# Full-width numerators and a matmul queue that stays in its row mode, in a linear-attention plus FFN kernel

## Chip, cores, metric

The kernel runs on one core of one Trainium2 chip. The metric is the device time of one execution in microseconds (us), as a median over runs. Runs of the kernel before lie within about 1 us of their median. All runs compared here are of the same ("fast") state unless a line says otherwise.

## The reference

Per batch (8) and head (8), queries, keys and values of 576 tokens x 64 go through a feature map and linear attention; the heads are joined to 4608 tokens x 512 and go through an FFN with a squared relu.

```python
def phi(x):
    proj = np.einsum('bhsd,df->bhsf', x, w_phi)            # 64 -> 128 features
    proj = proj - np.max(np.abs(proj), axis=-1, keepdims=True)
    return np.concatenate([np.exp(proj), np.exp(-proj)], axis=-1)
q_p, k_p = phi(q), phi(k)
kv  = np.einsum('bhsf,bhsd->bhfd', k_p, v)
num = np.einsum('bhsf,bhfd->bhsd', q_p, kv)
den = np.einsum('bhsf,bhf->bhs', q_p, np.sum(k_p, axis=2))[..., None] + 1e-06
x   = (num / den) ...                                     # (4608, 512)
h   = np.maximum(x @ w_in, 0.0)                           # d_ff = 2048
out = h * h @ w_out
```

## The kernel before

The kernel is a list of operations with keys (priorities), durations and dependencies. A planner in Python simulates the engines while the program is built and fixes the order of the instructions on each engine. The chip then runs that fixed order.

PE, the tensor engine, works in three shapes here: the FFN and the attention numerators contract over 128 rows; the projections of k and q and the k-v products contract over 64 rows (`rows=64`), two of them side by side in the array; and numerators of a lone half tile of 64 tokens use 128 rows x 64 columns ("column tiled"). The planner charges 96 ns when the row mode changes and nothing for a change of columns:

```python
    SWITCH = 96
    ...                                     # order(): PE picks the ready op of lowest key
                skip = []
                while q:
                    it = heapq.heappop(q)
                    o = it[2]
                    if not can(o):          # its PSUM banks or other buffers are not free
                        skip.append(it)
                        continue
    ...
                    if o.rows is not None:
                        if rows[e] not in (None, o.rows):
                            end += self.SWITCH
                        rows[e] = o.rows
```

PSUM, where PE's results land, is used as 8 banks (`r_one`). Attention may hold 6 at a time (`NATT = 6`), and a projection takes two, because it is written so that the two halves of the array write to different ones.

```python
    NATT, LEAD, DUE, SPAN = 6, 3, 34, 28
    r_one = ring("one", 8, [P, 512], F32, ps)
    r_att = Ring(list(range(NATT)))
    MARGIN = 300                            # added to the plan's latency of every eviction
    ...
            w, qg = banks(2), [Buf(r_qph), Buf(r_qph)]      # a q projection
    ...
            p_ = pe(kk, nj * 108, fn, tq + [o_wphi], w + [qT] + qg, 64)
```

Per batch there are 9 columns of 64 tokens: four pairs (`nj = 2`) and one single (`nj = 1`). The numerator of a single has 64 stationary columns and writes 64 PSUM partitions:

```python
            lo, hi_ = g0 % 2 * 64, (g0 % 2 + nj) * 64
    ...
                def nd(c, w=w, lo=lo, hi_=hi_):
                    return w.t.rearrange("t (h c) -> t h c", h=4)[lo:hi_, :, c]
                def fn(s, nd=nd, qg=qg, lo=lo, hi_=hi_, r=r):
                    for z in range(4):
                        h = 4 * r + z
                        nc.tensor.matmul(
                            out=nd(slice(0, D + 1))[:, z],
                            lhsT=qg[s].t.rearrange("f pr hi p -> f (pr hi p)")[
                                :, h * (hi_ - lo) : (h + 1) * (hi_ - lo)],
                            rhs=kv[r][0].t[:, z % 2, z // 2, s, :], ...)
```

An FFN unit is four 128x512 matmuls, 0.86 us. Attention operations become ready some three units before their key.

Of the kernel before, what the change touches and what calls it, by code (L numbers as in the profile page):

```python
# [17 lines left out]
class Buf:  # L18
# [5 lines left out]
    def can(self):  # L24
        free = self.ring.free
        return bool(free) if self.want is None else self.want in free
# [19 lines left out]
class Plan:  # L46
# [28 lines left out]

    SWITCH = 96

    def order(self):
        ready = {e: [] for e in sorted({o.eng for o in self.ops}, key=lambda e: (e != "x", e))}
        busy = {e: 0.0 for e in ready}  # L80
        rows = {e: None for e in ready}
        for o in self.ops:
            if o.n == 0:
                heapq.heappush(ready[o.eng], (o.key, o.seq, o))
        ev, now, done = [], 0.0, []

        def can(o):
            new = [x for x in o.bufs if x.slot is None]
            return all(x.can() and len(x.ring.free) >= sum(y.ring is x.ring for y in new)
                       for x in new)  # L90

        while True:
            for e, q in ready.items():
                if busy[e] > now:
                    continue
                skip = []
                while q:
                    it = heapq.heappop(q)
                    o = it[2]
                    if not can(o):  # L100
                        skip.append(it)
                        continue
                    for x in o.bufs:
                        if x.slot is None:
                            x.take()
                    o.start = now
                    end, lat = now + o.cost, o.lat
# [4 lines that stand above are left out]
                    busy[e] = end  # L112
                    done.append(o)
                    same = [d for d in o.next if d.eng == e]
                    other = [d for d in o.next if d.eng != e]
                    for i, (t, what) in enumerate((
                            (end, ()), (end + 60, same), (end + lat, other),
                            (end + lat, None))):
                        heapq.heappush(ev, (t, 4 * o.seq + i, o, what))
                    break  # L120
                for it in skip:
                    heapq.heappush(q, it)
                if busy[e] <= now and e in self.idle and self.idle[e][2].start is None:
                    cost, fn, _ = self.idle[e]
                    o = Op()
                    o.eng, o.fn, o.start, o.cost, o.key = e, fn, now, cost(now), 1e9
                    busy[e] = now + o.cost
                    done.append(o)
                    heapq.heappush(ev, (busy[e], -len(done), o, ()))
            if not ev:  # L130
                break
            now = ev[0][0]
            while ev and ev[0][0] <= now:
                _, _, o, what = heapq.heappop(ev)
                if what is None:
                    for x in o.bufs:
                        x.left -= 1
                        if x.left == 0:
                            x.ring.free.append(x.slot)
                    continue  # L140
                for d in what:
                    d.n -= 1
                    if d.n == 0:
                        heapq.heappush(ready[d.eng], (d.key, d.seq, d))
        assert all(o.start is not None for o in self.ops)
        self.span = now
        return done
# [10 lines left out]
def kernel(  # L158
# [12 lines left out]
    B, H, S, D = q.shape  # L171
    Fd = w_phi.shape[1]
    DM, DF = moe_w_in.shape
    P = 128
# [73 lines left out]
    def banks(n):  # L248

        w = [Buf(r_one) for _ in range(n)]  # L250
        for x in w:
            x.token = Buf(r_att)
        return w
# [25 lines left out]
    def begin():  # L279
# [5 lines left out]
        out=scrap[:, 4:8], in_=scrap[:, 0:4], func=ACT.Exp), [o_begin])  # L285
# [56 lines left out]
    def attention(b, x, key):  # L342
# [41 lines left out]
        if b:  # L384
            d = pl.op("x", 1000, key(2), None, tq)
            gates[b] = pool(key(2), 100, lambda: nc.gpsimd.tensor_copy(
                out=gate, in_=qT.t[:1, M - 1, P - 8 :]), [d], [qT])
# [4 lines left out]
        if b:  # L392
            def fn():
                nc.gpsimd.memset(va[0].t[:, :, D], 1.0)
                nc.gpsimd.tensor_copy(out=va[0].t[:, :, :D], in_=xv.t)
# [5 lines left out]
        for g, (u0, n) in enumerate(GRP):  # L401
            kk = key(2 + 8 * g)
            w = banks(2)
            c = n * 64
# [54 lines left out]
            for s_, (y, sg) in enumerate(zip(va, (-1.0, 1.0))):  # L459
# [4 lines left out]
                o = act(kk - 1, 2 * n, fn, d1, [y, mk])  # L464
# [11 lines left out]
        while g0 < (b + 1) * NJ:  # L476
            j0 = jord[b % 2][g0 - b * NJ]
            nj = 1 if j0 == NJ - 1 else 2
# [4 lines left out]
        for hf in range(2):  # L483
            t = Buf(r_kv)
            w = banks(2)

            def kvp(w, hi):
                return w[hi].t.rearrange("f (i c) -> f i c", i=4)[:, :, : D + 1]
            ops = []
            for prl in range(2):  # L490
                pr = 2 * hf + prl
# [17 lines left out]
            o = []  # L509
            for hi in range(2):  # L510
                kk = key(KV_AT[1] + 8 * hf + 6 if b else 20)
                if b or hi:
                    o.append(act(kk, 260, lambda w=w, t=t, hi=hi: nc.scalar.activation(
                        out=t.t[:, hi].rearrange("f pr s c -> f (pr s) c"),
                        in_=kvp(w, hi), func=ACT.Copy), ops, w + [t]))
                else:
                    o.append(dve(kk, 260, lambda w=w, t=t, hi=hi: nc.vector.tensor_copy(
                        out=t.t[:, hi].rearrange("f pr s c -> f (pr s) c"),
                        in_=kvp(w, hi)), ops, w + [t]))
# [5 lines left out]
        for i, (g0, j0, nj) in enumerate(order_j):  # L525
            lo, hi_ = g0 % 2 * 64, (g0 % 2 + nj) * 64
            kk = key(Q2_AT[b > 0][i])
            w, qg = banks(2), [Buf(r_qph), Buf(r_qph)]
# [15 lines left out]
            qe = []  # L544
            for bk in range(2):
                for t, sg in zip(qg, (1.0, -1.0)):
                    def fn(w=w, t=t, sg=sg, nj=nj, bk=bk):
                        nc.scalar.activation(  # L548
                            out=t.t.rearrange("f pr hi p -> f (pr hi p)")[:, : nj * 512].rearrange(
                                "f (r b c) -> f b r c", r=2, b=2)[:, bk],  # L550
                            in_=w[bk].t[:, : nj * 256].rearrange("f (r c) -> f r c", r=2),
                            func=ACT.Exp, scale=sg)
                    qe.append(act(kk, nj * 256, fn, [p_], [w[bk], t]))

# [2 lines left out]
            w, m0, mq, em = banks(2), Buf(r_m0), Buf(r_mq), Buf(r_em)  # L557

            def fn(w=w, j0=j0, nj=nj):
# [12 lines left out]
                out=m0.t[:, bk, : 2 * nj],  # L572
                in_=w[bk].t[:, : nj * 256].rearrange("x (i f) -> x i f", f=Fd),
# [23 lines left out]
            c, tt = tile_of[n2]  # L597
# [8 lines left out]
            for r in range(2):  # L606
                w, = banks(1)
                hs = slice(4 * r, 4 * r + 4)

                def nd(c, w=w, lo=lo, hi_=hi_):  # L610
                    return w.t.rearrange("t (h c) -> t h c", h=4)[lo:hi_, :, c]

                def fn(s, nd=nd, qg=qg, lo=lo, hi_=hi_, r=r):
                    for z in range(4):
                        h = 4 * r + z
                        nc.tensor.matmul(  # L616
                            out=nd(slice(0, D + 1))[:, z],
                            lhsT=qg[s].t.rearrange("f pr hi p -> f (pr hi p)")[
                                :, h * (hi_ - lo) : (h + 1) * (hi_ - lo)],
                            rhs=kv[r][0].t[:, z % 2, z // 2, s, :],  # L620
                            start=(s == 0 and z == 0), stop=True, skip_group_check=True)
                bs = [w, rd, xo, kv[r][0]]
                p_ = pe(kk, 132, lambda fn=fn: fn(0), [o_em] + qe + kv[r][1], bs + [qg[0]])

                def sc(nd=nd, em=em, lo=lo, hi_=hi_, hs=hs):
                    x = nd(slice(0, D + 1))
                    nc.vector.tensor_tensor(  # L627
                        out=x, in0=x, in1=em.t[lo:hi_, hs].to_broadcast(list(x.shape)),
                        op=ALU.mult)
                dk = kk - 20  # L630
                d_ = dve(dk, 260, sc, [p_, o_em], [w, em])
                p_ = pe(dk, 132, lambda fn=fn: fn(1), [d_], bs + [qg[1]])
                d_ = dve(dk, 50, lambda nd=nd, rd=rd, lo=lo, hi_=hi_, hs=hs:
                    nc.vector.reciprocal(out=rd.t[lo:hi_, hs], in_=nd(D)), [p_], [w, rd])

                def fn(nd=nd, rd=rd, xo=xo, lo=lo, hi_=hi_, hs=hs):
                    x = nd(slice(0, D))
                    nc.vector.tensor_tensor(  # L638
                        out=xo.t[lo:hi_].rearrange("t (h d) -> t h d", h=H)[:, hs],
                        in0=x, in1=rd.t[lo:hi_, hs].to_broadcast(list(x.shape)), op=ALU.mult)  # L640
                parts.append(dve(dk, 250, fn, [d_], [w, rd, xo]))
            nds.append(p_)
            if hi_ == P and b == 0:
                w, = banks(1)
# [159 lines left out]
```

## Time and profile before

| | before |
|---|---|
| time, median of 3 | 383.3 us (382.87 to 383.75) |
| first matmul on wout (its load has landed) | 49.5 us into the span |
| last 64-row matmul (end of the projections) | 302.9 us |
| changes of row mode in the whole trace | 212 |
| changes of columns alone | 47 |

PE is busy nearly throughout; at first it fills its idle time with matmuls on `ones` whose result is not used. Once wout has landed, PE's own stream sets the time. "Busy" is not "useful", though: PE's records overlap, so a drained array is not seen as idle. It is seen in the start times. The timeline of PE before, where columns are start, duration, engine, line, operation, shapes and count:

```profile
66.83 0.44 PE L616 MATMUL one<-kv_sb,qph 128*64 128x65 bf16 x8
67.20 1.04 PE L708 MATMUL one<-wout,h 128*128 128x512 bf16 x4
68.17 0.39 PE L538 MATMUL one<-qT,wphi 64*128 64x256 bf16 x4
...
152.57 0.41 PE L616 MATMUL one<-kv_sb,qph 128*128 128x65 bf16 x8
152.81 1.02 PE L708 MATMUL one<-wout,h 128*128 128x512 bf16 x4
153.77 0.39 PE L538 MATMUL one<-qT,wphi 64*128 64x256 bf16 x4
...
165.46 0.40 PE L412 MATMUL one<-wphi,kT 64*128 64x128 bf16 x8
165.79 1.04 PE L679 MATMUL one<-xT,win 128*128 128x512 bf16 x4
166.76 0.40 PE L412 MATMUL one<-wphi,kT 64*128 64x128 bf16 x8
167.09 1.04 PE L679 MATMUL one<-xT,win 128*128 128x512 bf16 x4
168.06 0.29 PE L412 MATMUL one<-wphi,kT 64*128 64x128 bf16 x4
168.28 4.49 PE L679 MATMUL one<-xT,win 128*128 128x512 bf16 x20
```

Read the starts. Four 512-column matmuls take 4 x 0.216 = 0.86 us; but from 152.81 to the 64-row work at 153.77 it is 0.96, and from 67.20 to 68.17 it is 0.97: 0.1 us went into the change of mode. Eight column-tiled numerators at 66.83 take 0.37 us to the next start, eight full ones at 152.57 only 0.24. And at 165 to 168 us three k projections stand alone between single FFN units: six changes of mode within 3 us.

The two forms of numerator, and of their weight loads, in the groups by form of the kernel before (after the bar: busy us and mean ns; then idle time before them):

```profile
L616 PE MATMUL one<-kv_sb,qph 128*128 128x65 bf16 x512 | 28.5, 195 | 1.5 <-DVE one L627 1.4
L616 PE MATMUL one<-kv_sb,qph 128*64 128x65 bf16 x128 | 9.1, 200 | 0.0
...
L616 PEld LDWEIGHTS <-qph 128*128 128x128 bf16 x512 | 23.6, 98 | 13.6 <-issue 2.9
L616 PEld LDWEIGHTS <-qph 128*64 128x64 bf16 x128 | 6.1, 110 | 8.6 <-issue 8.5
```

The durations look alike (195 and 200 ns): the cost is not in the matmul but around it. The Trainium skill, "TensorEngine Tiling (Array Packing)", Restrictions and Gotchas, says that column tiling excludes Fast Weight Load; the 64-column loads at 110 ns against 98 for full ones fit that, but weakly: the full loads of the filler matmuls average 106, and nothing here shows the mode bit.

### The profile page before, as it was taken

To read this page: it belongs to the slowest core of one execution; us is meant where nothing else is said; L and a number is where in the kernel's file an instruction comes from. 1 tells how busy PE (TensorE), PEld (TensorE's weight loads), DVE (VectorE), ACT (ScalarE), POOL (GpSimd) and SP (SyncE) were. 2 spreads that over 40 slices of the span, in tenths; PEclk is the share of its full clock that TensorE was granted. 3 is DMA by queue.
4 is the path that set the end of the run, shared out by engine and by line. 5 is a ranking of instruction groups with operands and counts; after the bars stand their busy time and mean duration, and the time that the engine had idled before them with its cause. 6 is when DMAs were issued, how large, how long until landed. Compare 5 with 4: busy or idle time off the path is not lost.

```text
span 382.5 us, 10585 instructions
## 1 busy us (share of the span) xinstructions
PE 366.7 (96%) x4194; PEld 200.9 (53%) x4194; DVE 247.7 (65%) x554; ACT 244.4 (64%) x485; POOL 185.9 (49%) x317
## 2 busy tenths in 40 slices
PE   8989999978999999999999999999999999999994
PEld 8868857544544454545543544455446444444442
DVE  1857894899279738973699488956895843333221
ACT  3785788649972986489758974996399733333300
POOL 8533766507890986079728674677446420000000
PEclk9998999999999999999999999999999999999998
DMA  7999994257944595459665946495631422112123
GB/s 114 213 208 205 162 174 73 48 91 133 195 50 89 91 217 62 80 105 202 99 85 109 169 85 104 91 196 102 105 77 30 71 55 49 35 29 55 27 64 75
DMA packets 70721, 40.41 MB, mean 106 GB/s; under 512 B 51088, under 2 KB 65552, under 8 KB 70672
## 3 DMA queue, kind: packets, MB, share of 16 engines
q1 hardware_dynamic: 55360, 21.38, 31.2%
q0 software_dynamic: 15312, 18.35, 29.4%
q8 instruction: 33, 0.54, 0.6%
q14 instruction: 16, 0.13, 0.1%
HBM read 36.77 MB, written 9.44 MB: 121 GB/s over the span
## 4 chain that ended last, share of the span: by engine, by line
PE 74%; DMA 11%; DVE 9%; issue 3%; POOL 1%; DVEq 0%; POOLq 0%
PE one L708 32%; PE one L679 25%; DMA wout<-in_moe_w_out_dram 8%; PE one L616 5%; PE one L500 5%; DVE mk L423 4%; DVE ksh L433 3%; PE one L538 3%; DMA xv<-in_v_dram 2%; PE one L567 2%; PE one L412 2%; DVE ot L715 1%; DVE xo L638 1%; POOL va L467 1%; DVE one L627 1%
## 5 line engine op out<-in xcount | busy, mean ns | idle before, releaser
L687 POOL TENSOR_TENSOR h<-hr 128x512 bf16<-128x512 bf16 x112 | 115.2, 1042 | 83.7 <-ACT hr L684 81.7
L679 PE MATMUL one<-xT,win 128*128 128x512 bf16 (+2 forms) x704 | 144.2, 341 | 2.8 <-DVE ksh L433 2.8
L708 PE MATMUL one<-wout,h 128*128 128x512 bf16 x576 | 144.5, 380 | 0.8 <-DMA wout<-in_moe_w_out_dram 0.5
L684 ACT ACTIVATE hr<-one 128x512 bf16<-128x512 f32 x144 | 84.5, 603 | 67.7 <-PE one L679 59.8
L548 ACT ACTIVATE qph<-one 128x512 bf16<-128x512 f32 (+1 forms) x160 | 77.9, 563 | 19.5 <-PE one L538 19.3
L679 PEld LDWEIGHTS <-win 128*128 128x128 bf16 x704 | 59.2, 98 | 54.6 <-issue 3.5
L708 PEld LDWEIGHTS <-h 128*128 128x128 bf16 x576 | 51.0, 98 | 56.6 <-issue 1.4
L441 ACT ACTIVATE kph<-ksh 128x1024 bf16<-128x1024 f32 (+1 forms) x70 | 64.8, 964 | 19.7 <-DVE ksh L433 19.2
L571 DVE TENSOR_REDUCE m<-one 128x4 f32<-128x512 f32 (+1 forms) x80 | 47.9, 630 | 41.7 <-PE one L567 24.9
L423 DVE TENSOR_REDUCE mk<-one 128x4 f32<-128x512 f32 (+1 forms) x80 | 49.7, 627 | 8.3 <-PE one L412 8.2
L433 DVE TENSOR_TENSOR ksh<-one,mk 128x512 f32<-128x512 f32 (+1 forms) x70 | 44.7, 638 | 3.8
L715 DVE COPY ot<-one 128x512 f32<-128x512 f32 x36 | 24.7, 685 | 28.2 <-PE one L708 28.0
L580 POOL COPY mq<-m 64x4 f32<-64x4 f32 x144 | 26.5, 184 | 32.0 <-DVE m L571 27.3
L616 PEld LDWEIGHTS <-qph 128*128 128x128 bf16 (+1 forms) x640 | 29.7, 100 | 22.2 <-issue 11.3
L616 PE MATMUL one<-kv_sb,qph 128*128 128x65 bf16 (+1 forms) x640 | 36.9, 196 | 1.5 <-DVE one L627 1.4
L627 DVE TENSOR_TENSOR one<-one,em 128x260 f32<-128x260 f32 (+1 forms) x80 | 31.5, 429 | 5.8 <-PE one L616 2.3
L638 DVE TENSOR_TENSOR xo<-one,rden 128x256 bf16<-128x256 f32 (+1 forms) x80 | 31.7, 419 | 0.8
L690 DVE TENSOR_TENSOR h<-hr 128x512 bf16<-128x512 bf16 x32 | 13.5, 423 | 24.4 <-ACT hr L684 24.4
L323 PE MATMUL one<-ones 128*128 128x128 bf16 x316 | 24.0, 236 | 1.1 <-DVE scrap L281 1.1
L500 PE MATMUL one<-va,kph 64*128 64x65 bf16 x1152 | 22.8, 191 | 0.9 <-issue 0.9
L500 PEld LDWEIGHTS <-kph 64*128 64x128 bf16 x1152 | 20.5, 94 | 4.3 <-issue 3.3
L323 PEld LDWEIGHTS <-ones 128*128 128x128 bf16 x316 | 20.6, 106 | 2.5 <-DVE scrap L281 1.1
(43 smaller groups left out, 184.5 us busy)
## 6 DMA issues: line engine op xcount, KB each, us to landing
out_dram<-ot SPq DMA_DIRECT2D x72, 128.0 KB, 2.4
xk<-in_k_dram POOLq DMA_DIRECT2D x7, 576.0 KB, 6.1
xq<-in_q_dram POOLq DMA_DIRECT2D x7, 576.0 KB, 9.8
xv<-in_v_dram POOLq DMA_DIRECT2D x7, 576.0 KB, 12.2
win<-in_moe_w_in_dram POOLq DMA_DIRECT2D x1, 2048.0 KB, 18.5
wout<-in_moe_w_out_dram POOLq DMA_DIRECT2D x1, 2048.0 KB, 32.4
xk<-in_k_dram POOLq DMA_DIRECT2D x2, 288.0 KB, 5.6
xq<-in_q_dram POOLq DMA_DIRECT2D x2, 288.0 KB, 7.6
```

The source lines that it names most:

```text
L323: nc.tensor.matmul(out=r_one.tiles[7][:, :P], lhsT=ones, rhs=ones, start=True, stop=True)
L423: nc.vector.tensor_reduce(out=mk.t[:, e, ms], in_=wv(e), axis=AX.X, op=ALU.max, apply_absolute_value=True)
L433: nc.vector.tensor_tensor(out=ksh.t[:, e, : n // 2, :], in0=wv(e), in1=mk.t[:, e, ms].to_broadcast([P, n // 2, Fd]), op=ALU.subtract)
L441: nc.scalar.activation(out=t.t[:, :, : n // 2, :].rearrange("x e i f -> x e (i f)"), in_=ksh.t[:, :, : n // 2, :].rearrange("x e i f -> x ...
L500: nc.tensor.matmul(out=kvp(w, hi)[:, 2 * prl + s], lhsT=kph[g][s].t[r, i % 2, i // 2, :], rhs=va[s].t[r, u, : D + 1], start=(j == 0), stop ...
L548: nc.scalar.activation(out=t.t.rearrange("f pr hi p -> f (pr hi p)")[:, : nj * 512].rearrange("f (r b c) -> f b r c", r=2, b=2)[:, bk], in ...
L571: d1 = [dve(kk, nj * 256, lambda w=w, m0=m0, nj=nj, bk=bk: nc.vector.tensor_reduce(out=m0.t[:, bk, : 2 * nj], in_=w[bk].t[:, : nj * 256].r ...
L616: nc.tensor.matmul(out=nd(slice(0, D + 1))[:, z], lhsT=qg[s].t.rearrange("f pr hi p -> f (pr hi p)")[:, h * (hi_ - lo) : (h + 1) * (hi_ - ...
L679: nc.tensor.matmul(out=w.t[:, y * n : (y + 1) * n], lhsT=win[:, kc, mc * P : (mc + 1) * P], rhs=xT.t[:, a:z, kc, :], start=(kc == 0), stop ...
L684: o = act(key - 4, TCH, lambda: nc.scalar.activation(out=r.t, in_=w.t, func=ACT.Relu), [p_], [w, r])
L687: o = pool(key - 4, 1050, lambda: nc.gpsimd.tensor_tensor(out=t.t, in0=r.t, in1=r.t, op=ALU.mult), [o], [r, t])
L708: nc.tensor.matmul(out=w.t, lhsT=h2[c, mc, tt][0].t[:, h2[c, mc, tt][1] :][:, :P], rhs=wout[:, mc, :], start=(mc == 0), stop=(mc == KC2 - 1))
```

## The change

Its intent is twofold. Numerators of single half tiles become full 128x128 matmuls: the exponentials go to their own 64 columns of a full-width tile (`lo:hi_`), the other columns hold what an earlier tile left, and the rows of the result that come from these are never read. And PE's queue prefers work in the row mode that the array is in: once in 64-row mode it goes on with ready 64-row work (up to 12 keys ahead); in 128-row mode it goes over only for two overdue operations, or one that is 8 keys late.

```diff
+    AHEAD, GROUP, LATE = 12, 2, 8
+
+    def pick(self, q, rows, can):
+        now = min((it[0] for it in q if it[2].rows == 128), default=None)
+        half = sorted(it for it in q if it[2].rows == 64 and can(it[2]))
+        if now is None or now < 1 or not half:
+            return None                                  # the old rule
+        if rows == 64:
+            go = half[0][0] < now + self.AHEAD
+        else:
+            go = half[0][0] < now - self.LATE or (
+                len([it for it in half if it[0] < now]) >= self.GROUP)
+        if go:
+            one = half[0]
+        else:
+            one = min((it for it in q if it[2].rows == 128 and can(it[2])), default=None)
+            if one is None:
+                return None
...
-                while q:
-                    it = heapq.heappop(q)
-                    o = it[2]
+                one = self.pick(q, rows[e], can) if e == "pe" else None
+                while q or one:
+                    it = one or heapq.heappop(q)
+                    one, o = None, it[2]
...
-                            out=t.t.rearrange("f pr hi p -> f (pr hi p)")[:, : nj * 512].rearrange(
-                                "f (r b c) -> f r b c", r=2, b=2)[:, bk],
+                            out=t.t.rearrange("f (r b) hi p -> f b r hi p", b=2)[:, bk, :, :, lo:hi_],
...
-                            out=nd(slice(0, D + 1))[:, z],
-                            lhsT=qg[s].t.rearrange("f pr hi p -> f (pr hi p)")[
-                                :, h * (hi_ - lo) : (h + 1) * (hi_ - lo)],
+                            out=w.t[:, z * P : z * P + D + 1],
+                            lhsT=qg[s].t[:, h // 2, h % 2, :],
```

More of the change, by code (lines that the diff above doesn't have):

```diff
@@ L76 @@
     SWITCH = 96
+    AHEAD, GROUP, LATE = 12, 2, 8
[15 more added lines that the diff above has]
+                return None
+        q.remove(one)
+        heapq.heapify(q)
+        return one
     def order(self):
@@ L546, in attention, with fn @@
                 for t, sg in zip(qg, (1.0, -1.0)):
-                    def fn(w=w, t=t, sg=sg, nj=nj, bk=bk):
+                    def fn(w=w, t=t, sg=sg, nj=nj, bk=bk, lo=lo, hi_=hi_):
                         nc.scalar.activation(
-                            out=t.t.rearrange("f pr hi p -> f (pr hi p)")[:, : nj * 512].rearrange(
-                                "f (r b c) -> f b r c", r=2, b=2)[:, bk],
-                            in_=w[bk].t[:, : nj * 256].rearrange("f (r c) -> f r c", r=2),
+                            out=t.t.rearrange("f (r b) hi p -> f b r hi p", b=2)[:, bk, :, :, lo:hi_],
+                            in_=w[bk].t[:, : nj * 256].rearrange(
+                                "f (r hi c) -> f r hi c", r=2, hi=2),
                             func=ACT.Exp, scale=sg)
@@ L611, in nd, with fn @@
                     return w.t.rearrange("t (h c) -> t h c", h=4)[lo:hi_, :, c]
-                def fn(s, nd=nd, qg=qg, lo=lo, hi_=hi_, r=r):
+                def fn(s, w=w, qg=qg, r=r):
                     for z in range(4):
```

## The prediction

> **What bounds the kernel now.** PE does. The page gives PE 96% of a 382.5 us span; by windows it is about 98% busy from 100 to 250 us and 100% from 250 to 350 us. The chain of waits agrees: PE 74%, and 11% DMA, which lies at the start (wout lands at 49.4 us; until then PE runs 316 filler matmuls on `ones`).  So about 49 us stay; the other 333 us are PE's stream, and what shortens it shortens the kernel.
>
> **What a mode change costs.** From the start times of successive matmuls in the trace: a 128x512 matmul is followed by another of the same mode after 216 ns, by a 64-row matmul after 312 ns, and by a 128x64 (column-tiled) matmul after 309 ns: 96 and 93 ns more. Back again: a 64-row matmul of 128 columns is followed by a 128-row one after 148 ns, where about 56 is its own work; a column-tiled one by a full one after 128 ns, against 32 for a full matmul of 65 columns. So each change, in either direction and of either kind, costs about 95 ns. The Trainium skill, "TensorEngine Tiling (Array Packing)", Key Properties, says that changing the mode drains the engine; the trace agrees and gives the 95 ns. The planner charges nothing for a column change.
>
> After 50 us the trace has 184 row changes (92 stretches of 64-row work, 17.5 us) and 47 changes of columns alone (4.5 us).
>
> **What the change does.**
> 1. Column tiling goes. The 128 matmuls of 64 columns (numerators of single half tiles, 8 of 40 tiles) become full ones over partly stale weights; the count stays at 640. Saved: 47 changes x 95 ns = 4.5 us, and 37 to 31 ns apart for some hundred = 0.6 us.
> 2. The queue groups 64-row work. In the timeline most stretches are a single projection of 0.22 to 0.33 us between one or a few FFN units (five for the k projection of each batch, about as many for the q projections). Waiting for two overdue ones and then draining what is ready should pair these. Each takes 2 of 6 banks, so more than three in a row are rare. I estimate 13 stretches per paced batch falling to about 8: 92 to about 57, 70 changes x 95 ns = 6.7 us.
>
> All of this is on PE's chain after 50 us. Nothing is saved before.
>
> Given back: waits on evictions. After 50 us, gaps of over 0.3 us between matmuls sum to about 10 us. Bunched projections fill the banks at once, so this may move by 2 or 3 us either way; I add nothing.
>
> **Prediction.** 383.3 - 5.1 - 6.7 = 371.5 us, range 366 to 378. Faster by over 2% 0.78, within 2% 0.20, slower 0.02.
>
> **What would show it.** No 128x64 form in the PE groups; the numerators one form, x640. 50 to 65 stretches of 64-row work after 50 us, each change still about 95 ns. wout's landing still near 49 us. The last attention work ends earlier, by roughly 12 us (before: 313 us), and the FFN-only tail stays as long (about 69 us).
>
> **What would make it wrong.** The banks allow only one projection at a time, so stretches stay above 80 and only the column part (5 us, 1.3%) is left; or bunching makes PE wait on DVE and ACT by several us.

One slip in it: the times that it reads from start times (50 us and 313 us) count from the first record of the trace, 10.5 us ahead of the span's start. On the span's clock they are 39.5 and 302.9 us. Counts and costs are not touched by this; below, all times are on the span's clock. Another slip: the filler matmuls do not run until wout lands (49.4 us), the last of them starts at 35.8 us.

## More of the kernel before

From the page of the kernel before: the busy line, and PE and its granted clock in 40 slices (tenths).

```profile
span 382.5 us, 10585 instructions
...
PE 366.7 (96%) x4194; PEld 200.9 (53%) x4194; DVE 247.7 (65%) x554; ACT 244.4 (64%) x485; POOL 185.9 (49%) x317
...
PE   8989999978999999999999999999999999999994
...
PEclk9998999999999999999999999999999999999998
...
PE 74%; DMA 11%; DVE 9%; issue 3%; POOL 1%; DVEq 0%; POOLq 0%
```

The last line is the chain of work that ended last.

## The result

| | before | after |
|---|---|---|
| time, median (4 runs each) | 383.52 us (382.87 to 384.66) | 377.51 us (376.50 to 378.81) |
| ratio of fast runs | 1 | 0.984, 95% interval 0.981 to 0.987 |
| row changes, whole trace | 212 | 196 |
| row changes, from 39.5 us on | 184 | 166 |
| changes of columns alone | 47 | 0 |
| first matmul on wout | 49.5 us | 48.3 us |
| last 64-row matmul | 302.9 us | 301.2 us |

A ratio is the mean time of one kernel's fast runs over that of the other's of the same rounds, so it is not quite the ratio of the medians. The change gains 1.6%, 6 us where 11.8 were forecast. From the page after:

```profile
span 375.1 us, 10592 instructions
...
PE 362.0 (97%) x4194; PEld 202.3 (54%) x4194; DVE 249.2 (66%) x554; ACT 244.0 (65%) x485; POOL 186.2 (50%) x317
...
PE   8979999979899999999999999999999999999994
...
PEclk9998999997999999999999999999999999999998
...
PE 85%; DVE 6%; DMA 4%; issue 2%; ACT 1%; POOL 0%; SPq 0%; DVEq 0%; ACTq 0%; POOLq 0%
```

Two things to see. PE is still the chain. And the granted clock, which before was full from 32 us to the last few, has a dip in the tenth slice (84 to 94 us). The numerators now have one form, in the groups by form after:

```profile
L639 PE MATMUL one<-kv_sb,qph 128*128 128x65 bf16 x640 | 35.9, 194 | 0.4 <-DVE one L649 0.4
```

And grouping does occur in the timeline of PE after: three k projections in a row, where before they stood alone.

```profile
156.16 2.75 PE L701 MATMUL one<-xT,win 128*128 128x512 bf16 x12
158.84 0.84 PE L435 MATMUL one<-wphi,kT 64*128 64x128 bf16 x24
159.62 1.04 PE L730 MATMUL one<-wout,h 128*128 128x512 bf16 x4
```

It is rarer than forecast: 16 changes fewer in all.

To see where time went, I split the start-to-start times of PE's matmuls from 49.5 us to the last matmul: full-mode work at its own pace (216 ns at 512 columns), the usual pace within 64-row stretches, up to 96 ns for each change of mode, what passed beyond that (waits), and what passed beyond it while the trace shows the clock at half. Both traces are complete (576 matmuls on wout). The terms depend on the paces that one takes for usual: a recount with others moved single terms by up to 5 us, but kept the changes between the two kernels within 1 us of those shown. All in us:

| stretch of the span | | own work, full | own pace, 64 rows | row changes | column changes | waits | clock at half | sum |
|---|---|---|---|---|---|---|---|---|
| 49.5 to 110 | before | 40.9 | 8.1 | 4.4 | 1.1 | 5.9 | 0 | 60.3 |
| | after | 39.4 | 8.0 | 4.3 | 0 | 6.1 | 2.8 | 60.6 |
| 110 to the end | before | 222.4 | 22.5 | 12.2 | 3.3 | 6.9 | 0 | 267.3 |
| | after | 222.5 | 22.9 | 10.8 | 0 | 3.6 | 0 | 259.8 |

The late part gained 7.5 us: 3.3 from columns, 1.4 from rows, 3.3 from fewer waits. That is all of the 7.4 us between the two spans: at 110 us both kernels have the same full-mode work left (222.4 and 222.5 us). So the early part gained nothing, although the changed kernel used wout 1.2 us sooner (this varies between executions: e1 below, with the old order, also shows 48.2) and saved 1.1 us of column changes. Both went into a new loss, 2.8 us at half clock.

Here is that spell in the timeline of PE after; brackets give idle time before an instruction and what ended it.

```profile
80.30 0.28 PE L639 MATMUL one<-kv_sb,qph 128*128 128x65 bf16 x4 [0.35 <-DVE one L649]
80.52 0.40 PE L435 MATMUL one<-wphi,kT 64*128 64x128 bf16 x8
80.97 0.28 PE L639 MATMUL one<-kv_sb,qph 128*128 128x65 bf16 x4
81.18 0.23 PE L435 MATMUL one<-wphi,kT 64*128 64x128 bf16 x1
82.28 0.38 PE L435 MATMUL one<-wphi,kT 64*128 64x128 bf16 x7 [0.87 <-DVE ksh L456]
83.63 5.28 PE L701 MATMUL one<-xT,win 128*128 128x512 bf16 x12 [0.97 <-DVE xo L660]
```

The same place in the timeline of PE before:

```profile
84.42 0.40 PE L412 MATMUL one<-wphi,kT 64*128 64x128 bf16 x8
85.52 2.75 PE L679 MATMUL one<-xT,win 128*128 128x512 bf16 x12 [0.70 <-DVE ksh L433]
```

In both kernels PE waits there for DVE, which has the k features to shift and the numerators to scale. In the changed one the 12 matmuls that follow take 5.28 us instead of 2.75. The trace's clock record says why: half clock from 82.8 us for 6.8 us.

### The profile page after: what moved, and what is told of

Read it like the earlier page. It is cut to its first block, busy times and chain, and to the rows that moved or that the text cites. A ratio compares the mean times of both kernels' runs of the same rounds, so it can differ in the third digit from the quotient of the medians.

```text
span 375.1 us, 10592 instructions
## 1 busy us (share of the span) xinstructions
PE 362.0 (97%) x4194; PEld 202.3 (54%) x4194; DVE 249.2 (66%) x554; ACT 244.0 (65%) x485; POOL 186.2 (50%) x317
## 4 chain that ended last, share of the span: by engine, by line
PE 85%; DVE 6%; DMA 4%; issue 2%; ACT 1%; POOL 0%; SPq 0%; DVEq 0%; ACTq 0%; POOLq 0%
PE one L730 31%; PE one L701 31%; PE one L523 5%; PE one L639 5%; PE one L346 4%; PE one L590 3%; PE one L561 3%; PE one L435 2%; DVE mk L446 2%; DMA xq<-in_q_dram 2%; DVE ksh L456 2%; DMA out_dram<-ot 1%; DVE xo L660 1%; DVE one L649 1%; PE one L387 1%
## 5 line engine op out<-in xcount | busy, mean ns | idle before, releaser
L701 PE MATMUL one<-xT,win 128*128 128x512 bf16 (+2 forms) x704 | 147.4, 345 | 1.4 <-DVE xo L660 1.0
L706 ACT ACTIVATE hr<-one 128x512 bf16<-128x512 f32 x144 | 85.7, 604 | 72.5 <-PE one L701 62.0
L701 PEld LDWEIGHTS <-win 128*128 128x128 bf16 x704 | 60.0, 98 | 55.2 <-issue 5.6
L571 ACT ACTIVATE qph<-one 128x512 bf16<-128x512 f32 (+1 forms) x160 | 77.8, 577 | 11.8 <-PE one L561 11.5
L737 DVE COPY ot<-one 128x512 f32<-128x512 f32 x36 | 24.7, 687 | 26.7 <-PE one L730 25.1
L639 PEld LDWEIGHTS <-qph 128*128 128x128 bf16 x640 | 30.8, 98 | 18.1 <-issue 2.4
L639 PE MATMUL one<-kv_sb,qph 128*128 128x65 bf16 x640 | 35.9, 194 | 0.4 <-DVE one L649 0.4
L523 PE MATMUL one<-va,kph 64*128 64x65 bf16 x1152 | 22.0, 190 | 1.2 <-issue 1.2
L523 PEld LDWEIGHTS <-kph 64*128 64x128 bf16 x1152 | 20.0, 94 | 4.7 <-issue 4.2
```

The lines of the kernel that those rows point to most:

```text
L523: nc.tensor.matmul(out=kvp(w, hi)[:, 2 * prl + s], lhsT=kph[g][s].t[r, i % 2, i // 2, :], rhs=va[s].t[r, u, : D + 1], start=(j == 0), stop ...
L571: nc.scalar.activation(out=t.t.rearrange("f (r b) hi p -> f b r hi p", b=2)[:, bk, :, :, lo:hi_], in_=w[bk].t[:, : nj * 256].rearrange("f ...
L639: nc.tensor.matmul(out=w.t[:, z * P : z * P + D + 1], lhsT=qg[s].t[:, h // 2, h % 2, :], rhs=kv[r][0].t[:, z % 2, z // 2, s, :], start=(s ...
L701: nc.tensor.matmul(out=w.t[:, y * n : (y + 1) * n], lhsT=win[:, kc, mc * P : (mc + 1) * P], rhs=xT.t[:, a:z, kc, :], start=(kc == 0), stop ...
L706: o = act(key - 4, TCH, lambda: nc.scalar.activation(out=r.t, in_=w.t, func=ACT.Relu), [p_], [w, r])
```

## The experiments

Theory 1: the column part does what was forecast; the grouping falls short, because a projection needs two PSUM banks and attention's six are nearly always taken (theory A below). Rivals: the full-width matmuls have a cost of their own; a change of mode costs less of the kernel's time than of the trace; or the entry rule is at fault (theory B). Theory C: the new order lost time at 80 to 100 us. All kernels gave correct results.

### Each part alone

e1, the changed kernel with the old queue; PE's order is then exactly that of before:

```diff
-                one = self.pick(q, rows[e], can) if e == "pe" else None
+                one = None
```

> Only the column part: the queue is the old one, so the instruction order is that of before and the 92 stretches of 64-row work stay. My theory (the column part does what was forecast and the grouping fell short) expects 5 us less than before, ratio 0.987, about 378.5 us, no column changes left and 180 or so row changes after 50 us. The rival (the full matmuls cost something of their own, and the grouping is where the gain lies) expects under 2 us, ratio over 0.995.

Measured: 379.27 us (378.78 to 379.45), ratio 0.989 (0.987 to 0.990), that is 4.3 us less; no column changes, 212 row changes. The column part did nearly what was forecast (5.1), and the first rival is out.

e2, the kernel before with only the queue of the change (`pick` and its call).

> Only the queue: column tiling stays, so its changes stay. My theory expects 1.5 to 2.5 us less than before (8 or 9 stretches fewer at 2 x 95 ns, give or take a wait), ratio 0.994 to 0.996. The rival expects 4 us or more, ratio under 0.99. The two parts should add up to the change's 6 us within 1.5 us.

Measured: 382.04 us (380.31 to 386.11) over all six runs; the longest is slow and is not used, and the median of the five fast ones is 381.77. The ratio is 0.9945 (0.992 to 0.997): 2.1 us less, or 1.8 by the fast median; 196 row changes. By the ratios the two parts (4.4 and 2.1) add up to 6.5 us against the 6.1 of the change. So the shortfall is the grouping's: 6.7 us forecast, about 2 found. But its runs spread over 2 us even among the fast ones, and e1's over 0.7, which theory C would explain.

### What a change of mode costs in the kernel's time

Ahead of each of the 16 FFN-in units of the last chunk, long after the attention, ten extra 128-column matmuls write the unit's own bank, which the unit's first real matmul then overwrites. In e5 all are full; in e6 every second one has 64 rows; in e7 every second one has 64 columns. The order of all else is that of the changed kernel.

```diff
         def fn():
+            if c == 8:
+                for _ in range(5):
+                    nc.tensor.matmul(out=w.t[:, :P], lhsT=win[:64, 0, :P], rhs=win[:64, 1, :P], start=True, stop=True)   # e6
+                    nc.tensor.matmul(out=w.t[:, :P], lhsT=win[:, 0, :P], rhs=win[:, 1, :P], start=True, stop=True)
             for y in range(per):
```

> The changed kernel with 10 extra full 128x128 matmuls ahead of each of the 16 FFN-in units of the last chunk, which lie after the attention (the result stays right: the unit's first real matmul overwrites). No mode change: 160 x 56 ns = 9.0 us more than the changed kernel, about 386 us.

> The same, but every second extra matmul has 64 rows: 160 row changes. If a row change costs 95 ns of the kernel's time, 15.2 us more than the run with full extras, about 401 us. If the change is mostly hidden behind other latencies when the time is measured end to end, under 8 us.

> The same, but every second extra matmul has 64 columns: 160 column changes. 95 ns each gives 15.2 us more than the run with full extras, about 401 us, equal to the row changes within 2 us. A rival, that column changes cost less than row changes, expects under 10 us.

Measured: 387.18, 403.24 and 404.34 us. e5 came 1.2 us above its forecast (386). Against e5, 160 row changes cost 16.1 us (100 ns each) and 160 column changes 17.2 us (107 ns each). e5's own runs spread over 5 us, so by the intervals of the ratios these prices are good to about 18 and 24 ns. In the timeline of PE, first e5, then e6, then e7:

```profile
339.64 0.22 PE L701 MATMUL one<-win 128*128 128x128 bf16 x1
339.70 0.22 PE L700 MATMUL one<-win 128*128 128x128 bf16 x1
339.76 0.22 PE L701 MATMUL one<-win 128*128 128x128 bf16 x1
```

```profile
339.12 0.23 PE L701 MATMUL one<-win 128*128 128x128 bf16 x1
339.28 0.23 PE L700 MATMUL one<-win 64*128 64x128 bf16 x1
339.44 0.23 PE L701 MATMUL one<-win 128*128 128x128 bf16 x1
```

```profile
340.71 0.23 PE L701 MATMUL one<-win 128*128 128x128 bf16 x1
340.87 0.24 PE L700 MATMUL one<-win 128*64 128x128 bf16 x1
341.04 0.23 PE L701 MATMUL one<-win 128*128 128x128 bf16 x1
```

Starts 0.06 us apart became 0.16 and 0.16 to 0.17. The forecast's price of 95 ns holds within that, for rows and columns alike, and is paid in full where PE is the limit. The Trainium skill, "TensorEngine Tiling (Array Packing)", Key Properties, says that changing the tiling mode drains the engine; these runs agree. What was wrong was the number of changes, not their price.

### Why so few groups form

The order is fixed when the kernel is built, so the planner can be asked directly. In the changed kernel 82 stretches of 64-row work begin after the planner's first 40 us. Of their 82 ends, 67 come with 64-row work ready and no bank for any of it (in 1 more, other buffers are missing); in 13 none is ready; in 1 it is too far ahead. At 60 of the 82 beginnings only two or three of the six banks are free: room for one projection. `GROUP = 2` counts operations each of which could start alone. Given 14 banks and 12 for attention, the same rule lays out 55 stretches in the whole order instead of 91 (99 before), and 46 instead of 82 after the first 40 us, more grouping than the forecast's 57 asked for. That is a count of an order and not a time; no such program was run.

e3 asks for four free banks before a group is entered (theory B's cure):

```diff
             go = half[0][0] < now - self.LATE or (
+                len(self.banks.free) >= 4 and
                 len([it for it in half if it[0] < now]) >= self.GROUP)
```

> The changed kernel, but the queue enters 64-row mode for a group only when 4 of the 6 attention banks are free, so that two projections fit. Theory A (the banks are busy nearly all the time, so waiting for four only shifts the shortage elsewhere) expects the stretches to fall by 4 or so and the time by under 1.5 us against the changed kernel: ratio to before 0.980 to 0.984. Theory B (the entry rule is at fault, it counts projections that cannot both have banks) expects 15 or more stretches fewer and 3 us: 0.976 or under.

Measured: 379.99 us (378.99 to 382.50), ratio 0.992 (0.989 to 0.995). Row changes fell by 8 to 188, as theory A had it (4 stretches), but the time rose by 2 to 3 us against the changed kernel (ratios 0.984 and, in a repetition below, 0.987), which neither theory expected. Its profile shows waits inside 64-row stretches of 9.1 us from wout's first use on, against 4.6 in the changed kernel's first profile. The largest part of them is not a wait of projections for their evictions: 4.9 us, in three waits, lie in the k-v products (L525), where the changed kernel has 1.2 (L523), and the profile names no releaser ("issue"). More on this wait stands at the end of the waits under "The spell at 80 to 100 us".

e12 goes all the way: a group is entered only with six free banks, and lateness hardly overrides (`LATE = 99`). These are two edits, and neither does it alone: asked again, the planner gives 97 stretches with the six banks only and 87 with `LATE = 99` only, against 64 with both.

> The changed kernel, but a group of 64-row work is entered only when all 6 attention banks are free, and lateness hardly ever overrides that: 64 stretches in the order against 91. Theory A (the banks are the limit: groups can be had only by leaving banks empty) expects row changes to fall to about 110 after 50 us, worth 4 to 5 us, and the kernel to be slower than before all the same, 390 us or more, because the attention falls behind and FFN units wait for xT. If switches were what matters most and banks had slack, it would be 372 or less.

Measured: 417.36 us (414.79 to 418.44), ratio 1.086. Row changes fell to 142 (110 from wout's first use on), which is worth 4.8 us against the changed kernel's 160 there, and the kernel became 40 us slower. By stretches of the profile of e12 (PE, PEld, DVE, ACT, POOL busy us with counts; then the granted clock, DMA share and GB/s):

```profile
80.00:100.00 20.00, 9.71 (x86) 5.68 (x83) 17.14 (x36) 8.44 (x13) 4.07 (x12) 0.50 1.03 155
100.00:200.00 100.00, 88.96 (x918) 45.52 (x917) 55.13 (x124) 59.06 (x116) 56.61 (x92) 0.90 0.58 102
```

And three of PE's waits in e12 (engine and line, what it waited for; us in total, times, longest):

```profile
PE one L641 <- DVE one L651: 6.1, 7, 1.4
...
PE one L703 <- DMA xT<-xo: 5.4, 1, 5.4
...
PE one L703 <- ACT hr L708: 3.8, 4, 1.3
```

PE starves: FFN-in (L703) waits 5.4 us for an attention result, and the clock sits at half from 79.0 us for 23.9 us. So theory A stands for this way of grouping: to wait until banks are empty costs far more than the changes that it saves. That there is no other way is not shown; a smaller margin, below, removes changes without loss of time.

### The margin on evictions

If the plan frees a bank sooner, it can group more. e4 is e3 with `MARGIN = 0` in place of 300.

> As the run before, and the planner's 300 ns margin on each eviction is taken as 0, so that in the plan a bank comes free earlier. The order then has about 17 stretches fewer than the changed kernel. If the bank's time of occupation in the plan is what limits grouping, row changes fall to about 130 after 50 us, worth 3 us; if the margin stood for real latencies, PE's waits on DVE and ACT grow by as much or more. I expect 0.975 to 0.985 of before, and PE waits of 3 us more than in the changed kernel.

Measured: 377.03 us (375.14 to 378.10), ratio 0.982 (0.979 to 0.985). Row changes fell to 168 (132 from 39.5 us on, as expected), 28 below the changed kernel's 196 and worth 2.7 us, but the time is that of the changed kernel within noise. Its profile shows half clock twice, 3.4 us at 48.5 and 6.8 us at 82.7 us.

### The spell at 80 to 100 us

e8 keeps the old queue until key 30 rather than key 1. PE's order is then that of before up to 101 us of its profile (not about 85, as the text below says), through the whole spell, and groups after that. The whole order has 91 stretches, as many as the changed kernel.

```diff
-        if now is None or now < 1 or not half:
+        if now is None or now < 30 or not half:
```

> The changed kernel, but the queue keeps its old rule until key 30, so PE's order is that of before up to about 85 us, and groups after that; the number of 64-row stretches in the whole order is the same as in the changed kernel. Theory C (the changed order leaves PE nearly idle around 80 to 84 us, where its clock is then halved, and that gives back 1.5 to 3 us and makes the times spread) expects no halved clock between 50 and 110 us, a spread of the runs under 1.5 us as in the column-only kernel, and 1 to 2.5 us less than the changed kernel of the same rounds: about 375.5. The rival (the halved clock is an accident that costs nothing in the end, being hidden by later slack) expects the changed kernel's time within 0.5 us.

The changed kernel was run again beside it:

> The changed kernel itself, to compare with the three on the same chip: 376.5 to 378.8, ratio 0.982 to 0.987, and a halved clock between 80 and 100 us in its profile in most cases.

Measured: e8 373.81 us (373.25 to 374.32), ratio 0.975 (0.974 to 0.976); the changed kernel 378.89 us (375.99 to 380.77), ratio 0.987 (0.983 to 0.990), 0.1 us above what was expected of it, with half clock at 92.3 us. Their row changes are the same, 196 each. So e8 is 5.1 us faster than the changed kernel of the same rounds by the medians (4.5 by the ratios, 3.5 against the changed kernel's first ratio of 0.984), about twice what was expected, and its runs spread over 1.1 us where those of the changed kernel spread over 4.8. By stretches: the kernel before, the changed kernel, its repetition (e11), and e8.

```profile
80.00:100.00 20.00, 16.61 (x213) 8.13 (x213) 15.99 (x33) 15.65 (x25) 10.76 (x19) 1.00 0.78 144
```

```profile
80.00:100.00 20.00, 16.60 (x220) 7.82 (x220) 14.20 (x28) 16.21 (x28) 12.05 (x21) 0.83 0.92 161
```

```profile
80.00:100.00 20.00, 15.03 (x174) 7.11 (x173) 14.64 (x30) 15.66 (x25) 11.00 (x19) 0.91 0.91 166
```

```profile
80.00:100.00 20.00, 16.61 (x240) 8.41 (x237) 13.65 (x27) 17.84 (x32) 12.32 (x21) 1.00 0.86 155
```

PE's busy time is the same in three and 1.6 us less in e11; its clock differs, and so does the number of matmuls got through (240 in e8, 174 in e11). Split as above, from wout's first use to 110 us, full-mode work done was 41.3 us in e8, 39.4 in the changed kernel's first profile and 37.3 in e11 (the traces of e8 and e11 lack some 40 of the 576 matmuls on wout, so their figures are rough). Half clock accounts for 0, 2.8 and 1.5 us of it, and waits inside 64-row stretches for 1.6, 3.1 and 6.8 us. The profiled execution of e8 is 3.2 us shorter than the first and 6.1 us shorter than e11 (spans 371.9, 375.1 and 378.0); so the early work explains 1.9 of 3.2 and 4.0 of 6.1. The rest lies later, where the order of e8 is a different one too.

Half clock is not the whole loss. In e6, whose order up to its last chunk is that of the changed kernel, the profile shows no half clock there, and 5.3 us of waits inside 64-row stretches all the same. Of the six profiles with the changed order in this stretch (the changed kernel twice, e2 in its slow run, e5, e6, e7), five show half clock between 80 and 110 us; of the three with the old order there (before, e1, e8), none does. Over all ten runs of the changed kernel, the three with a mean granted clock of 0.995 took 376.9 us on average and the seven with 0.983 to 0.991 took 378.7; e8's four, at 0.987 to 0.999, show no such trend. So the clock may be worth some 2 us, an estimate from these means.

Nor is PE's thin stretch there new. Within each trace the half clock begins on a fixed grid of 3.41 us. Counting matmuls at their usual pace, 20 of the 21 grid windows that a half clock followed (all 14 traces, from 5 us to the last matmul) hold 1.30 us of work or less and one holds 1.50; the windows under full clock that none followed hold 1.34 or more, but for one of 1.14. The old order has stretches of 3.41 us with 0.65 us of work too (before, from 82.1 us), as thin as the changed kernel's 0.68; in the three profiles no grid window fell on them. Taking 1.30 us for the limit, nearly half of the possible positions of the grid would have halved the clock there too (an estimate, 45% for each of the three traces). So the three clean profiles are partly luck.

What the waits are can be read in part. In all six profiles with the changed order the copy of a result to `ot` (L737 in the kernel after), which frees a bank, waits 0.9 to 2.8 us for an earlier store of `ot` to land, and in five of them PE then waits for that copy; in the three with the old order the copy does not wait. From the waits between 74 and 105 us, two lines of e11, then one of e8:

```profile
PE one L561 <- DVE ot L737: 1.8, 1, 1.8
DVE ot L737 <- DMA out_dram<-ot: 1.7, 1, 1.7
```

```profile
PE one L561 <- DVE ot L737: 0.3, 1, 0.3
```

All six also have a wait of 0.7 to 2.6 us within the k-v products (L523) that the profile puts to "issue". Of all "issue" waits of PE over 0.45 us in the 14 traces (15 after the first 47 us, e3's three among them), 14 end 1.2 to 1.6 us after a 16 KB transfer of DMA queue q8, kind "instruction", has ended. That fits PE waiting for its next instructions; no run tests it.

e9 and e10 add to the idea of e8 (old queue until key 40) the four banks of e3 and a margin of 0 and 150.

> Old rule until key 40, then grouping that waits for four free banks, and no margin on evictions in the plan: 71 stretches in the order against 91 of the changed kernel. If the stretches count at 2 x 95 ns each and waits do not grow, 3.8 us less than the changed kernel plus what theory C gives: 372 to 373. If the waits grow with it as in the run with margin 0 before, 375 to 377.

> The same with half the margin: 77 stretches. Between the two: 373 to 375.5.

Measured: e9 374.67 us (373.46 to 375.05), ratio 0.977; e10 375.01 us (374.59 to 376.40), ratio 0.979. Row changes are 162 and 170, 34 and 26 fewer than in e8, worth 3.2 and 2.5 us, and yet neither is faster than e8. Both profiles have half clock at 83 to 89 us again (e10 also at 48.1). e9 lies between its two expectations, e10 within its own. These runs change three things against e8 at once, so that a smaller margin pays for its fewer changes in waits and clock is a reading of the profiles and not shown; e8 stays the best version, 2.5% under before and 1.2% under the changed kernel by the ratios of the same rounds (0.975 over 0.987).

## Why the prediction was right or wrong

- **PE bounds it, and a change of mode costs 95 ns**: right. The runs with extra changes give 100 and 107 ns of kernel time each, give or take some 20.
- **Column part, 5.1 us**: right within 1 us. All 47 changes went; alone it gave 4.3 us.
- **Row part, "92 to about 57, 70 changes x 95 ns = 6.7 us"**: this is the step that failed. It was 92 to 83, 18 changes, 1.7 us at that price; alone it gave about 2 us. The prediction saw the cause ("The banks allow only one projection at a time, so stretches stay above 80") and put it among what could go wrong, reckoning that with six banks two or three projections would fit. It did not ask how many banks are free at the moment of choice: two or three at 60 of 82 beginnings. Nor did it count: the planner lays out the order without the chip, and gives 91 stretches against 99 before.
- **"I add nothing" for waits**: the net was small and hid two large terms. From 110 us on waits fell by 3.3 us; at 80 to 100 us the new order brought waits and a halved clock. e8, which keeps the old order up to 101 us, is 3.5 to 5 us faster than the changed kernel, though part of that lies later.
- **Attention ends 12 us earlier and the tail keeps its length**: wrong. The last 64-row matmul came 1.7 us earlier (302.9 to 301.2), while the rest after it shrank from 79.6 to 73.9 us of span. PE does more FFN before that point: the 577th of the 704 FFN-in matmuls started 8.6 us earlier (308.4 to 299.8 us).
- **The size**: 371.5 us was said, 377.5 came, at the edge of the range of 366 to 378. That it fell inside was luck: the repetition's median, 378.9, lies outside. The chance of 0.78 for over 2% was too high: the ratio was 0.984.

What stays open: why the same order waits 3.1 us within 64-row stretches in one execution and 6.8 in another (the landing of a store accounts for 1.8 us of it and the wait in the k-v products for 1.0, but why these vary is not known); and how much of e8's gain is the clock and how much the waits, since no experiment took one away without the other.

## What to carry to other kernels

Count changes of the array's mode and price them from start times, not from busy time; columns count like rows. Before expecting work to be grouped, look at what each piece needs at the moment of choice (here two PSUM banks of six), and where a planner fixes the order, count the groups in it before the forecast: a rule that groups work whose buffers are taken only changes the order. And where a new order is good in the main, look for the one stretch where the tensor engine runs thin: there the old order may be worth keeping, as e8, which kept it, was 3.5 to 5 us faster here.

## What the Trainium skill lacked or had wrong

- "TensorEngine Tiling (Array Packing)", Key Properties: it says that changing the mode drains the engine, but gives no price, and does not say whether columns cost what rows do. Here each change costs 93 to 96 ns between starts on the way in (312 and 309 ns against 216), and 100 (rows) and 107 ns (columns) of kernel time, good to about 18 and 24 ns.
- "TensorE: Matmul & The Clock Gate", Part 1: it gives half clock after at least one idle window of about 3.4 us. Here the records of half clock mostly last 3.4 us or twice that, which agrees; but the engine was not idle before: in the 3.41 us before the half clock at 82.8 us the changed kernel ran 29 matmuls, 1.05 us of work at their usual pace. How thin is too thin, the page does not say; in these traces the line lies near 1.3 us of work in a window of 3.41 (20 of 21 windows before a half clock hold 1.30 or less), with two windows on the wrong side of it, 1.14 and 1.50.
